# Batch 0 of a clustered-attention and MLP kernel: pieces placed by a table, and another start of head 0

## The chip, the cores and the metric

The kernel runs on one core of one Trainium2 chip. The metric is the device time of one execution in microseconds (us). The profile shows five engines of this core: TensorE (PE in the profile, its weight loads as PEld), VectorE (DVE), ScalarE (ACT), GpSimd (POOL) and SyncE (SP, which issues transfers here). In this kernel TensorE's results stand in PSUM tiles, and VectorE and ScalarE copy them to SBUF.

Kernels are compared only within the same rounds. A ratio is the mean time of one kernel's fast runs over the mean of the other's fast runs of the same rounds, so it is not quite the ratio of the medians that stand beside it.

## The reference

```python
q_n, k_n, c_n = (x / (norm(x) + 1e-6) for x in (q, k, centroids))
q_assign = argmax(einsum('bhsd,hcd->bhsc', q_n, c_n), -1)     # 16 clusters per head
k_assign = argmax(einsum('bhsd,hcd->bhsc', k_n, c_n), -1)
scores = q @ k.T / 8;  scores = where(q_assign == k_assign, scores, -1e9)
x = softmax(scores) @ v                    # 4 batches, 8 heads, 768 tokens, 64 wide
out = gelu_exact(x @ w_in) @ w_out         # 3072 tokens, 512 -> 2048 -> 512
```

There are 32 heads (4 batches of 8). Heads 0 to 9 are prepared with transposes on TensorE; later ones use transfers that transpose.

## The kernel before

Each head goes through these pieces. The names in brackets are those of the table that the change brings in.

- **Split** (GpSimd): q and k become a float16 high part and a float16 residual, side by side in `st`.
- **Transposes** (`trq`, `trk`): six on TensorE for each of q and k into a PSUM buffer, which VectorE copies to `T`.
- **Assignment** (`asq`, `ask`): `T` against the normalised centroids on TensorE.
- **One-hots** (`oneh`): on VectorE a sum of two halves, a maximum and a comparison.
- **One-hot rows** (`onep`): six transposes on TensorE and two VectorE writes into 16 extra rows of `T`, so that the score matmul adds a large value where clusters match.
- **Six key chunks** ("slots" (head, chunk)): two score matmuls, one exp on ScalarE. There are two score buffers in PSUM, so TensorE can be one slot ahead.
- **AV** (`av0` to `av5`): six matmuls each, in the next head's slots. Then **norm** on VectorE, and for each pair of heads **fin** (six transposes, one copy).

```python
def asn(i, which, halves=True):          # asq / ask
    ...
    for j in range(N):
        if halves:                       # both centroid halves side by side: 6 matmuls
            nc.tensor.matmul(a_ps[:, j, which], t[:, js], c_all[:, :, chs], start=True, stop=True)
        else:                            # accumulated: 12 matmuls, but no sum on VectorE
            for e in range(2):
                nc.tensor.matmul(a_ps[:, j, which, 0], t[:, js], c_all[:, e, chs],
                                 start=(e == 0), stop=(e == 1))

def onehot(i, halves=True):              # oneh
    ...
    if halves:
        nc.vector.tensor_reduce(out=asum, in_=..., op=ALU.add)      # the sum
    nc.vector.tensor_reduce(out=amax, in_=asum, op=ALU.max)
    nc.vector.tensor_tensor(oh[...], asum, amax..., op=ALU.is_ge)

def scores(i, c):
    s_ps = ps_sc.tile([128, 2, 512], FP32, tag="sc", name="sc_ps")   # ps_sc: two buffers
    for t in range(2):
        nc.tensor.matmul(s_ps[:, t, 0:QB], Ts[i][0:D + C, 1, ...], Ts[i][0:D + C, 0, ...], ...)
    nc.scalar.activation(ps[i][:, c, :], s_ps[...], ACT_FN.Exp, ...)

# ... the start
nc.gpsimd.tensor_tensor(cent_norm, cent_ssq, half, op=ALU.pow)
nc.vector.tensor_sub(sts[0][:, 1, :, D:2 * D], k_raw, sts[0][:, 1, :, 0:D])   # k residual, head 0
tr_pe(0, 0, copy=nc.scalar.copy, ...)
nc.vector.tensor_scalar_add(cent_norm, cent_norm, 1e-6)
nc.vector.reciprocal(cent_rnorm, cent_norm)
nc.vector.tensor_scalar_mul(cent_hl[:, 0], cent_sb..., cent_rnorm)            # "the multiply"
nc.vector.scalar_tensor_tensor(cent_hl[:, 1, 0, :], cent_sb, cent_rnorm, ...)
# ... placing the pieces, in units of a modelled slot time
AVS0 = {2: (0,), 3: (1, 2), 4: (3,), 5: (4, 5)}      # AV pieces of head i-1 in slot (i, c)
at(g(h - 2, 0), tr_pe, h, 0); at(g(h - 2, 2), tr_pe, h, 1)
at(g(h - 2, 4), prep_asn, h); at(g(h - 1, 1), one_pe, h)
```

The transposes, the one-hot rows and all fins but one share one ring of two PSUM buffers (`ps_o`). Assignment has one buffer and AV has one.

The softmax here doesn't subtract the row's maximum and nothing guards it: scores larger than these inputs give would overflow.

Of the kernel before, what the change touches and what calls it, by code (L numbers as in the profile page):

```python
# [9 lines left out]
FP16 = mybir.dt.float16  # L10
AX = mybir.AxisListType
ALU = mybir.AluOpType
# [8 lines left out]
def kernel(  # L21
# [10 lines left out]
    nc = tc.nc  # L32
# [3 lines left out]
    B, H, S, D = q.shape  # L36
    HC, C, _ = centroids.shape
    DM, DF = moe_w_in.shape
    N = S // 128
    NH = B * H  # L40
    QB = S // 2
# [17 lines left out]
    ps_sc = ctx.enter_context(tc.tile_pool(name="ps_sc", bufs=2, space=PSUM))  # L59
    ps_a = ctx.enter_context(tc.tile_pool(name="ps_a", bufs=1, space=PSUM))  # L60
    ps_x = ctx.enter_context(tc.tile_pool(name="ps_x", bufs=1, space=PSUM))
# [34 lines left out]
    def warm(n, cols=512):  # L96
        for _ in range(n):
            nc.tensor.matmul(w_ps[:, 0:cols], ones[:, 0:128], ones[:, 0:cols],  # L98
                             start=True, stop=True)
# [47 lines left out]
    def tr_pe(i, w, copy=None, pool=None):  # L147
        if i not in Ts:
            Ts[i] = t_pool.tile([128, 2, S], FP16, tag="T", name="T")
        st = sts[i]  # L150
        pl, tag = pool or (ps_o, "op")
        t_ps = pl.tile([128, S], FP16, tag=tag, name="tr_ps")
        for j in range(N):
            nc.tensor.transpose(t_ps[:, j * 128:(j + 1) * 128], st[:, w, j, :], ident)  # L154
        (copy or nc.vector.tensor_copy)(Ts[i][:, w, :], t_ps)  # L155
# [18 lines left out]
    sts[1] = st_pool.tile([128, 2, N, 2 * D], FP16, tag="st", name="st")  # L174
    vraws[1] = v1_raw
    nc.gpsimd.tensor_tensor(cent_norm, cent_ssq, half, op=ALU.pow)
    nc.vector.tensor_sub(sts[0][:, 1, :, D:2 * D], k_raw, sts[0][:, 1, :, 0:D])

    tr_pe(0, 0, copy=nc.scalar.copy, pool=(ps_sc, "sc"))
    warm(1, 256)  # L180
    nc.vector.tensor_scalar_add(cent_norm, cent_norm, 1e-6)
    nc.vector.reciprocal(cent_rnorm, cent_norm)
    nc.vector.tensor_scalar_mul(cent_hl[:, 0],
                                cent_sb.unsqueeze(1).to_broadcast([H * C, 2, D]), cent_rnorm)
    nc.vector.scalar_tensor_tensor(cent_hl[:, 1, 0, :], cent_sb, cent_rnorm,
                                   cent_hl[:, 0, 0, :], ALU.mult, ALU.subtract)
    nc.gpsimd.tensor_copy(half[:, 0:1], cent_hl[:, 1, 0, 0:1])
# [3 lines left out]
    def cent_tr():  # L191
        chl_ps = ps_a.tile([128, 2, 128], FP16, tag="asn", name="chl_ps")
        for w in range(2):
            nc.tensor.transpose(chl_ps[:, w], cent_hl[:, w].rearrange("p a d -> p (a d)"),
                                ident)
        nc.vector.tensor_copy(c_all, chl_ps)

    def tr(i):
        st = sts.pop(i)
# [9 lines left out]
    def asn(i, which, halves=True):  # L209
        h = i % H  # L210
        chs = slice(h * C, (h + 1) * C)
        if which == 0:
            asns[i] = ps_a.tile([128, 512], FP32, tag="asn", name="asn_ps")
        a_ps = asns[i][:, 0:2 * NA].rearrange("p (n w l c) -> p n w l c", n=N, w=2, l=2)
        t = Ts[i][:, which]
        for j in range(N):
            js = slice(j * 128, (j + 1) * 128)
            if halves:
                nc.tensor.matmul(a_ps[:, j, which], t[:, js], c_all[:, :, chs],  # L219
                                 start=True, stop=True)  # L220
            else:
# [4 lines that stand above are left out]
    def onehot(i, halves=True):  # L226
        tile_ps = asns.pop(i)
        a_ps = tile_ps[:, 0:2 * NA].rearrange("p (n w l c) -> p n w l c", n=N, w=2, l=2)
        oh = ohs[(i // 2) % NOH]
        if halves:  # L230
            asum = small.tile([128, N, 2, C], FP32, tag="asum", name="asum")
            nc.vector.tensor_reduce(out=asum, in_=a_ps.rearrange("p n w l c -> p n w c l"),  # L232
                                    axis=AX.X, op=ALU.add)
            amax = tile_ps[:, 2 * NA:2 * NA + 2 * N].rearrange("p (n w o) -> p n w o",
                                                               n=N, w=2)
        else:
            asum = a_ps[:, :, :, 0, :]
            amax = small.tile([128, N, 2, 1], FP32, tag="amax", name="amax")
        nc.vector.tensor_reduce(out=amax, in_=asum, axis=AX.X, op=ALU.max)  # L239
        nc.vector.tensor_tensor(oh[:, :, i % 2, :, 0:C], asum,  # L240
                                amax.to_broadcast([128, N, 2, C]), op=ALU.is_ge)
# [40 lines left out]
    def one_first():  # L282
        half_ps = []
        for e in range(2):
            t_ps = ps_o.tile([128, S], FP16, tag="op", name="oh_ps")
            for j in range(N // 2):
                nc.tensor.transpose(t_ps[:, j * 128:(j + 1) * 128],
                                    ohs[0][:, e * (N // 2) + j].rearrange("p a b c -> p (a b c)"),
                                    ident)
            half_ps.append(t_ps)  # L290
        one_q, one_k = half_ps
        T0 = Ts[0][D:D + C]
        nc.scalar.activation(T0[:, 0, QB:S], one_k[0:C, 0:QB], ACT_FN.Copy, bias=0.0,
                             scale=float(VAL))
        nc.vector.tensor_scalar(T0[:, 0, 0:QB], one_q[0:C, 0:QB],
                                float(VAL), None, op0=ALU.mult)
        for o, z in ((0, 128), (128, QB)):
            nc.vector.tensor_scalar(T0[:, 1, o:z], one_q[32:32 + C, o:z],
                                    -1.0, None, op0=ALU.add)
        tr_pe(1, 1, pool=(ps_x, "x"))  # L300
        nc.vector.tensor_scalar(T0[:, 1, QB:S], one_k[32:32 + C, 0:QB],
                                -1.0, None, op0=ALU.add)

# [118 lines left out]
        nc.gpsimd.dma_start(out=w_chunks[n][0], in_=w_chunks[n][1])  # L422


    tr_pe(0, 1, copy=nc.scalar.copy, pool=(ps_sc, "sc"))
    warm(1)
    nc.scalar.copy(sts[1][:, 1, :, 0:D], k1_raw)
    nc.gpsimd.tensor_sub(sts[1][:, 1, :, D:2 * D], k1_raw, sts[1][:, 1, :, 0:D])
    cent_tr()
    nc.vector.tensor_sub(sts[1][:, 0, :, D:2 * D], q1_raw, sts[1][:, 0, :, 0:D])  # L430
    warm(2)
    asn(0, 0, halves=False)
    asn(0, 1, halves=False)
    onehot(0, halves=False)
    warm(1)
    tr_pe(1, 0, copy=nc.scalar.copy, pool=(ps_sc, "sc"))
    one_first()
    split(2, vnow=False)
    load_w(0)
# [15 lines left out]

    WARM = {}
    AVS = {1: (0,), 2: (1,), 3: (2,), 4: (3,), 5: (4, 5)}
    AVS0 = {2: (0,), 3: (1, 2), 4: (3,), 5: (4, 5)}
    FILL = {}

    def slot(i, c):
        if i < NH:
            scores(i, c)
        if i in WARM:
            warm(WARM[i])
        fill(FILL.get((i, c), 2))
        if i >= 1:
            for j in (AVS0 if i < 10 else AVS).get(c, ()):
                av(i - 1, j)
            if c == 5:  # L470
                norm(i - 1)
# [8 lines left out]
    PT = 10  # L480
    FC1 = {(9, 3): 0, (18, 0): 1, (26, 0): 2}
    events = []

    def at(t, fn, *args, **kw):
        events.append((t, len(events), fn, args, kw))
# [33 lines left out]
    def g(i, c):  # L519
        return TS[i, c] + 0.01  # L520

    def prep_asn(h, halves=True):
        asn(h, 0, halves)
        asn(h, 1, halves)
        onehot(h, halves)

    for n in range(1, 8):
        at(T[n] + 0.5, load_w, n)
    sp_t = -3.7
# [8 lines left out]
            at(max(T[pair] - {10: 25.0, 12: 25.0, 14: 35.0}.get(pair, 29.0) + 2.5 * (h % 2), sp_t + 3.5), tr, h)  # L538
    for h in range(NH - 3, NH):
        at(sp_t + 0.04, vcast, h)  # L540
    for h in range(1, NH):
        pair = h - h % 2
        if h == 1:
            at(g(0, 0), asn, h, 0, False)
            at(g(0, 1), asn, h, 1, False)
            at(g(0, 1), onehot, h, False)
            at(g(0, 3), one_pe, h)
        elif h < PT:
            o = 4 if h == 2 else 0
            at(g(0, 4) if h == 2 else g(h - 2, 0), tr_pe, h, 0)  # L550
            at(g(0, 5) if h == 2 else g(h - 2, 2), tr_pe, h, 1)
            at(g(1, 1) if h == 2 else g(h - 2, 4), prep_asn, h, h > 2)
            at(g(h - 1, 1 + o // 2) if h < 11 else g(10, 4), one_pe, h)
        else:
            if pair < 10:
                at(g(pair - 2, 3) if h % 2 else g(pair - 3, 5), prep_asn, h)
                to, tg = T[pair] - g(pair - 2, 5), T[pair] - g(pair - 1, 2)
            else:
                ta, to, tg = (17.5, 12.0, 5.0) if pair >= 12 else (12.5, 7.0, 3.0)
                t0 = T[pair] - ta + 4.0 * (h % 2)  # L560
                at(t0, asn, h, 0)
                at(t0 + 1.2, asn, h, 1)
                at(t0 + 1.21, onehot, h)
            if h % 2 == 1:
                at(T[pair] - to, ohtr, pair)
                at(T[pair] - tg, aug, pair)
    for h in range(0, NH - 2, 2):
        if h < 8:
            at(g(h + 3, 3) if h < 6 else g(9, 1), fin, h, pe=True)
        else:  # L570
            at(T[h + 3] + 0.1, fin, h)

    for t, _, fn, args, kw in sorted(events, key=lambda e: e[:2]):
# [39 lines left out]
```

## Time and profile before

| | before |
|---|---|
| median of 3 runs, us | 302.93 (302.70 to 303.14) |
| span of the profiled run, us | 300.9 |
| first score matmul, us from the start | 9.39 |
| slots (2,0), (4,0), (6,0) start at | 18.92, 29.01, 38.73 |
| first MLP matmul | 55.52 |

"First MLP matmul" means here the first of the main MLP loop (`hp`, L386 in the kernel before). Eight early MLP matmuls (`hp_early`) are spread ahead of it, the first at 50.92 us.

Busy time of each engine in two stretches of the kernel before (the number in brackets counts instructions):

```profile
core 0: us, PE busy (x) PEld busy (x) DVE busy (x) ACT busy (x) POOL busy (x), PEclk, DMA share, GB/s
...
15.00:45.00 30.00, 29.82 (x512) 23.88 (x511) 26.21 (x59) 27.91 (x38) 28.77 (x45) 1.00 1.15 268
60.00:250.00 190.00, 190.00 (x1973) 117.46 (x1972) 71.98 (x171) 148.49 (x186) 53.80 (x85) 1.00 0.60 131
```

From 60 us on TensorE is busy without a break, so a shift of the first stretch should pass to the end. In batch 0 four engines look nearly full. For TensorE this is misleading. The Trainium skill ("TensorE: Matmul & The Clock Gate", section "Wait — 56ns, not 53.3ns?") gives a start-to-start time of 55.6 ns for warm back-to-back matmuls of 128 columns. The trace agrees: transposes recorded at 219 ns start every 55 ns, so most of the recorded time overlaps. A slot can then be summed by starts: two score matmuls 0.32 us, six AV matmuls 0.18, six transposes 0.34, twelve assignment matmuls 0.30.

This is the timeline of TensorE, then of ScalarE, around slot (5,3) of the kernel before. The columns are the start, the time to the end of the merged row, the engine, line, operation and operands, and in brackets the idle time before it and who ended it:

```profile
36.06 0.49 PE L311 MATMUL sc_ps<-T 80*128 80x384 f16 x2
36.39 0.53 PE L326 MATMUL x_ps<-vaug_149,p_sb 128*128 128x65 f16 x12
36.88 0.51 PE L350 MATMUL fin_ps<-ident,x_tok 128*128 128x128 f16 x6
37.22 0.49 PE L311 MATMUL sc_ps<-T 80*128 80x384 f16 x2
```

```profile
34.26 3.14 ACT L314 ACTIVATE p_sb<-sc_ps 128x768 f16<-128x768 f32 x4
37.75 2.37 ACT L314 ACTIVATE p_sb<-sc_ps 128x768 f16<-128x768 f32 x3 [0.35 <-PE sc_ps L311]
```

The slot holds twelve AV matmuls and six transposes. The next pair of score matmuls therefore starts 1.16 us later (36.06 to 37.22), where ScalarE needs a new one every 0.70 us, and ScalarE idles 0.35 us.

The start, on VectorE, in the kernel before:

```profile
3.73 0.56 DVE L163 TENSOR_TENSOR st<-q_raw,st 128x384 f16<-128x384 f32 x1
4.38 0.56 DVE L177 TENSOR_TENSOR st<-k_raw,st 128x384 f16<-128x384 f32 x1
4.85 0.15 DVE L181 TENSOR_SCALAR cent_norm<-cent_norm 128x1 f32<-128x1 f32 x1
5.04 0.16 DVE L182 RECIPROCAL cent_rnorm<-cent_norm 128x1 f32<-128x1 f32 x1
5.24 0.29 DVE L183 TENSOR_SCALAR cent_hl<-cent_sb,cent_rnorm 128x128 f16<-128x128 f32 x1
```

The k residual of head 0 (L177) stands ahead of the centroid chain; the multiply (L183) takes 0.29 us.

### The profile page before, as it was taken

Reading aid. Unit: us, or ns where it says so; the run is one execution under the profiler, and the core shown is the slowest. Engines: PE = TensorE matmul, PEld = TensorE weight load, DVE = VectorE, ACT = ScalarE, POOL = GpSimd, SP = SyncE. Lnnn points to the kernel's source line nnn. Section 1 sums busy time; section 2 is a strip of 40 time slices with the busy share of each in tenths; the row PEclk is TensorE's granted clock in tenths of the full one; section 3 lists DMA queues with packets and bytes.
Section 4 is the critical chain, followed back from the end, with each engine's and each line's share of the span. In section 5 each row is a group of like instructions: output and inputs, shape, how many; then the busy total and the mean of one; then the engine's idle time right before and its main releaser. Section 6 shows DMA issues by size and latency. Waiting matters only on the chain.

```text
span 300.9 us, 7413 instructions
## 1 busy us (share of the span) xinstructions
PE 295.8 (98%) x3109; PEld 186.8 (62%) x3109; DVE 122.8 (41%) x284; ACT 215.2 (72%) x274; POOL 106.6 (35%) x182
## 2 busy tenths in 40 slices
PE   8899999999999999999999999999999999999996
PEld 4678887666666666666566666666566665565444
DVE  5788987103564732122353842223344413000112
ACT  5899999956888888856788888855788883466000
POOL 3999999998033204663522304600000000000000
PEclk9999999999999999999999999999999999999999
DMA  6999999993378369976579436876032231100122
GB/s 232 361 297 254 259 262 210 237 233 87 60 178 206 91 81 238 232 160 178 113 162 197 118 86 209 165 96 131 2 89 54 70 54 44 38 0 0 44 97 70
DMA packets 74065, 42.85 MB, mean 142 GB/s; under 512 B 54320, under 2 KB 71088, under 8 KB 74032
## 3 DMA queue, kind: packets, MB, share of 16 engines
q1 hardware_dynamic: 69520, 38.09, 52.5%
q0 software_dynamic: 4224, 4.19, 8.4%
q8 instruction: 24, 0.39, 0.6%
q10 hardware_dynamic: 288, 0.10, 0.1%
q14 instruction: 9, 0.07, 0.1%
HBM read 27.30 MB, written 6.29 MB: 112 GB/s over the span
## 4 chain that ended last, share of the span: by engine, by line
PE 94%; POOL 2%; DVE 1%; ACT 1%; issue 0%
PE hp L386 27%; PE op L412 24%; PE sc_ps L311 20%; PE x_ps L326 11%; PE op_alt L412 3%; PE asn_ps L219 3%; PE tr_ps L154 2%; PE w_ps L98 1%; PE oh_ps L265 1%; PE fin_ps L350 1%; POOL st L133 1%; ACT p_sb L314 1%; ACT T L155 1%; PE hp_early L367 0%; POOL st L132 0%; POOL st L135 0%
## 5 line engine op out<-in xcount | busy, mean ns | idle before, releaser
L314 ACT ACTIVATE p_sb<-sc_ps 128x768 f16<-128x768 f32 x192 | 148.9, 810 | 21.8 <-PE sc_ps L311 12.9
L311 PE MATMUL sc_ps<-T 80*128 80x384 f16 x384 | 93.7, 325 | 0.7 <-ACT p_sb L314 0.4
L386 PE MATMUL hp<-xt,w_in_sb 128*128 128x384 f16 x504 | 85.0, 326 | 0.0
L326 PEld LDWEIGHTS <-p_sb 128*128 128x128 f16 x1152 | 54.6, 97 | 30.9 <-DVE x_tok L337 0.2
L386 PEld LDWEIGHTS <-w_in_sb 128*128 128x128 f16 x504 | 47.9, 98 | 30.4
L132 POOL CAST st<-q_raw 128x384 f16<-128x384 f32 x30 | 15.3, 509 | 78.7 <-DMA q_raw<-in_q_dram 56.9
L416 DVE COPY o_sb<-op 128x512 f32<-128x512 f32 (+1 forms) x22 | 14.8, 672 | 54.9 <-PE op L412 54.9
L232 DVE TENSOR_REDUCE asum<-asn_ps 128x192 f32<-128x384 f32 x29 | 16.2, 557 | 51.3 <-PE asn_ps L219 51.2
L311 PEld LDWEIGHTS <-T 80*128 80x128 f16 x384 | 26.8, 97 | 5.5 <-issue 1.1
L135 POOL TENSOR_TENSOR st<-k_raw,st 128x384 f16<-128x384 f32 x30 | 27.4, 913 | 2.4
L133 POOL TENSOR_TENSOR st<-q_raw,st 128x384 f16<-128x384 f32 x30 | 27.3, 911 | 2.5
L336 DVE RECIPROCAL rec<-x_ps 128x6 f32<-128x6 f32 x32 | 6.2, 193 | 42.5 <-PE x_ps L326 42.5
L337 DVE TENSOR_TENSOR x_tok<-x_ps,rec 128x384 f16<-128x384 f32 x32 | 17.8, 558 | 1.1
L219 PEld LDWEIGHTS <-T 128*128 128x128 f16 x348 | 14.7, 96 | 4.4
L219 PE MATMUL asn_ps<-c_all,T 128*128 128x32 f16 x348 | 16.7, 177 | 0.0
L134 POOL CAST st<-k_raw 128x384 f16<-128x384 f32 x30 | 15.2, 505 | 0.0
L275 DVE TENSOR_SCALAR T<-ohT 16x768 f16<-16x768 f16 x22 | 8.2, 371 | 8.2 <-DMA ohT<-oh_166 4.0
L154 PE MATMUL tr_ps<-ident,st 128*128 128x128 f16 x120 | 10.6, 227 | 0.3 <-POOL st L133 0.2
L239 DVE TENSOR_REDUCE asn_ps<-asum 128x12 f32<-128x192 f32 x29 | 10.5, 361 | 1.0
L154 PEld LDWEIGHTS <-st 128*128 128x128 f16 x120 | 8.6, 101 | 3.1 <-DVE st L163 0.9
L155 DVE COPY T<-tr_ps 128x768 f16<-128x768 f16 x17 | 9.4, 554 | 0.6
L278 DVE TENSOR_SCALAR T<-ohT 16x768 f16<-16x768 f16 x22 | 9.0, 410 | 0.3
(308 smaller groups left out, 405.4 us busy)
## 6 DMA issues: line engine op xcount, KB each, us to landing
q_raw<-in_q_dram SPq DMA_DIRECT2D x32, 192.0 KB, 4.2
k_raw<-in_k_dram SPq DMA_DIRECT2D x32, 192.0 KB, 4.1
v_raw<-in_v_dram SPq DMA_DIRECT2D x32, 192.0 KB, 4.0
out_dram<-o_sb SPq DMA_DIRECT2D x23, 256.0 KB, 2.3
w_in_sb<-in_moe_w_in_dram POOLq DMA_DIRECT2D x4, 512.0 KB, 9.5
w_out_sb<-in_moe_w_out_dram POOLq DMA_DIRECT2D x4, 512.0 KB, 9.9
T<-st SPq DMA_TRANSPOSE x22, 4.8
xt<-x_tok SPq DMA_TRANSPOSE x11, 2.9
```

What stands on the lines that cost most here:

```text
L132: nc.gpsimd.tensor_copy(st[:, 0, :, 0:D], q_raw)
L133: nc.gpsimd.tensor_sub(st[:, 0, :, D:2 * D], q_raw, st[:, 0, :, 0:D])
L135: keng.tensor_sub(st[:, 1, :, D:2 * D], k_raw, st[:, 1, :, 0:D])
L154: nc.tensor.transpose(t_ps[:, j * 128:(j + 1) * 128], st[:, w, j, :], ident)
L219: nc.tensor.matmul(a_ps[:, j, which], t[:, js], c_all[:, :, chs], start=True, stop=True)
L232: nc.vector.tensor_reduce(out=asum, in_=a_ps.rearrange("p n w l c -> p n w c l"), axis=AX.X, op=ALU.add)
L311: nc.tensor.matmul(s_ps[:, t, 0:QB], Ts[i][0:D + C, 1, c * 128:(c + 1) * 128], Ts[i][0:D + C, 0, t * QB:(t + 1) * QB], start=True, stop=True)
L314: nc.scalar.activation(ps[i][:, c, :].rearrange("p (t q) -> p t q", t=2), s_ps[:, :, 0:QB], ACT_FN.Exp, bias=0.0, scale=float(scale))
L326: nc.tensor.matmul(x_ps[:, j], ps[i][:, ch, j * 128:(j + 1) * 128], va[:, ch, 0:D + 1], start=(ch == 0), stop=(ch == N - 1))
L337: nc.vector.tensor_tensor(xtoks[i - i % 2][:, :, i % 2, :], x_ps[:, :, 0:D], rec.to_broadcast([128, N, D]), op=ALU.mult)
L386: nc.tensor.matmul(hp[:, t, 0:QB], w_in_sb[:, m, f * 128:(f + 1) * 128], xts[b][:, m, t * QB:(t + 1) * QB], start=(m == 0), stop=(m == NM ...
L412: nc.tensor.matmul(op[:, 0:w], gs[b][f][:, js], w_out_sb[:, f, ms], start=(f == 0), stop=(f == NF - 1))
```

## The change

The intent is to fill the slots of batch 0 more evenly and to reach the first score sooner. The AV, transpose, assignment, one-hot, norm and fin pieces of heads 0 to 9 (AV and norm up to head 8) are listed per slot in a table. Head 0's k residual goes to GpSimd so that the centroids come sooner. Head 0's k transposes are evicted in two halves, one by ScalarE and one by VectorE. Head 1's k transposes move into the first slot. Head 2's assignment uses the form with 12 matmuls and a sum. In the diff, `warm(n)` issues n filler matmuls on TensorE whose results nobody reads; a pair of heads, below, is the time from slot (4,0) to slot (6,0).

```diff
-    nc.vector.tensor_sub(sts[0][:, 1, :, D:2 * D], k_raw, sts[0][:, 1, :, 0:D])
+    nc.gpsimd.tensor_sub(sts[0][:, 1, :, D:2 * D], k_raw, sts[0][:, 1, :, 0:D])
...
-    nc.vector.tensor_scalar_mul(cent_hl[:, 0],
-                                cent_sb.unsqueeze(1).to_broadcast([H * C, 2, D]), cent_rnorm)
+    nc.vector.tensor_tensor(cent_hl[:, 0], cent_sb.unsqueeze(1).to_broadcast([H * C, 2, D]),
+                            cent_rnorm.unsqueeze(2).to_broadcast([H * C, 2, D]), op=ALU.mult)
...
+    def tr_halves(i, w):
+        for e, (pl, tag, copy) in enumerate(((ps_sc, "sc", nc.scalar.copy),
+                                             (ps_o, "op", nc.vector.tensor_copy))):
+            ...   # three transposes and a copy of 384 columns each
...
-        tr_pe(1, 1, pool=(ps_x, "x"))
+        tr_pe(1, 0, pool=(ps_x, "x"))
...
-    tr_pe(0, 1, copy=nc.scalar.copy, pool=(ps_sc, "sc"))
     warm(1)
+    cent_tr()
+    tr_halves(0, 1)
     nc.scalar.copy(sts[1][:, 1, :, 0:D], k1_raw)
     nc.gpsimd.tensor_sub(sts[1][:, 1, :, D:2 * D], k1_raw, sts[1][:, 1, :, 0:D])
-    cent_tr()
-    nc.vector.tensor_sub(sts[1][:, 0, :, D:2 * D], q1_raw, sts[1][:, 0, :, 0:D])
-    warm(2)
+    warm(1)
     asn(0, 0, halves=False)
     asn(0, 1, halves=False)
     onehot(0, halves=False)
-    warm(1)
-    tr_pe(1, 0, copy=nc.scalar.copy, pool=(ps_sc, "sc"))
+    nc.vector.tensor_sub(sts[1][:, 0, :, D:2 * D], q1_raw, sts[1][:, 0, :, 0:D])
+    warm(3)
     one_first()
...
+    PLAN = {
+        (0, 0): ((1, 'trk'),),
+        (0, 1): ((1, 'asq'),),
+        (0, 2): ((1, 'ask'), (1, 'oneh'),),
+        ...
+        (4, 0): ((5, 'oneh'), (2, 'norm'), (6, 'trq'),),
+        (4, 1): ((5, 'onep'),),
+        (4, 2): ((3, 'av0'), (3, 'av1'),),
+        (4, 3): ((6, 'trk'), (6, 'asq'),),
+        (4, 4): ((3, 'av2'), (3, 'av3'), (6, 'ask'),),
+        (4, 5): ((3, 'av4'), (3, 'av5'),),
+        ...   # up to (10, 0)
+    }
```

More of the change, by code (lines that the diff above doesn't have):

```diff
@@ L196, in cent_tr @@
         nc.vector.tensor_copy(c_all, chl_ps)
+    def tr_halves(i, w):
+        for e, (pl, tag, copy) in enumerate(((ps_sc, "sc", nc.scalar.copy),
+                                             (ps_o, "op", nc.vector.tensor_copy))):
+            t_ps = pl.tile([128, S], FP16, tag=tag, name="tr_ps")
+            for j in range(N // 2):
+                nc.tensor.transpose(t_ps[:, j * 128:(j + 1) * 128],
+                                    sts[i][:, w, e * (N // 2) + j, :], ident)
+            copy(Ts[i][:, w, e * QB:(e + 1) * QB], t_ps[:, 0:QB])
     def tr(i):
@@ L457 @@
     AVS = {1: (0,), 2: (1,), 3: (2,), 4: (3,), 5: (4, 5)}
-    AVS0 = {2: (0,), 3: (1, 2), 4: (3,), 5: (4, 5)}
     FILL = {}
@@ L466, in slot @@
         fill(FILL.get((i, c), 2))
-        if i >= 1:
-            for j in (AVS0 if i < 10 else AVS).get(c, ()):
+        if i >= 10:
+            for j in AVS.get(c, ()):
                 av(i - 1, j)
@@ L482 @@
     events = []
+    ONE = {1}
+    PLAN = {
+        (0, 0): ((1, 'trk'),),
+        (0, 1): ((1, 'asq'),),
+        (0, 2): ((1, 'ask'), (1, 'oneh'),),
+        (0, 3): ((2, 'trq'),),
+        (0, 4): ((1, 'onep'),),
+        (0, 5): ((2, 'trk'), (2, 'asq'),),
+        (1, 0): ((3, 'trq'),),
+        (1, 1): ((2, 'ask'), (2, 'oneh'), (3, 'trk'),),
+        (1, 2): ((0, 'av0'), (0, 'av1'),),
+        (1, 3): ((0, 'av2'), (2, 'onep'),),
+        (1, 4): ((3, 'asq'), (3, 'ask'), (0, 'av3'), (3, 'oneh'),),
+        (1, 5): ((0, 'av4'), (0, 'av5'), (0, 'norm'),),
+        (2, 0): ((4, 'trq'),),
+        (2, 1): ((3, 'onep'),),
+        (2, 2): ((1, 'av0'), (1, 'av1'),),
+        (2, 3): ((4, 'trk'), (4, 'asq'),),
+        (2, 4): ((1, 'av2'), (1, 'av3'), (4, 'ask'),),
+        (2, 5): ((1, 'av4'), (1, 'av5'),),
+        (3, 0): ((4, 'oneh'), (1, 'norm'), (5, 'trq'),),
+        (3, 1): ((4, 'onep'),),
+        (3, 2): ((2, 'av0'), (2, 'av1'), (2, 'av2'),),
+        (3, 3): ((5, 'trk'), (5, 'asq'),),
+        (3, 4): ((0, 'fin'), (2, 'av3'), (5, 'ask'),),
+        (3, 5): ((2, 'av4'), (2, 'av5'),),
+        (4, 0): ((5, 'oneh'), (2, 'norm'), (6, 'trq'),),
[4 more added lines that the diff above has]
+        (4, 5): ((3, 'av4'), (3, 'av5'),),
+        (5, 0): ((6, 'oneh'), (3, 'norm'), (7, 'trq'),),
+        (5, 1): ((6, 'onep'),),
+        (5, 2): ((4, 'av0'), (4, 'av1'), (7, 'asq'),),
+        (5, 3): ((7, 'trk'), (4, 'av2'),),
+        (5, 4): ((2, 'fin'), (7, 'ask'),),
+        (5, 5): ((4, 'av3'), (4, 'av4'), (4, 'av5'),),
+        (6, 0): ((7, 'oneh'), (4, 'norm'), (8, 'trq'),),
+        (6, 1): ((7, 'onep'),),
+        (6, 2): ((5, 'av0'), (5, 'av1'),),
+        (6, 3): ((8, 'trk'), (5, 'av2'),),
+        (6, 4): ((5, 'av3'), (8, 'asq'), (8, 'ask'),),
+        (6, 5): ((8, 'oneh'), (5, 'av4'), (5, 'av5'), (5, 'norm'),),
+        (7, 0): ((9, 'trq'),),
+        (7, 1): ((8, 'onep'),),
+        (7, 2): ((6, 'av0'), (6, 'av1'),),
+        (7, 3): ((9, 'trk'), (9, 'asq'),),
+        (7, 4): ((6, 'av2'), (6, 'av3'), (9, 'ask'),),
+        (7, 5): ((6, 'av4'), (9, 'oneh'), (6, 'av5'),),
+        (8, 0): ((6, 'norm'), (4, 'fin'),),
+        (8, 1): ((9, 'onep'),),
+        (8, 2): ((7, 'av0'), (7, 'av1'),),
+        (8, 3): ((7, 'av2'),),
+        (8, 4): ((7, 'av3'), (7, 'av4'),),
+        (8, 5): ((7, 'av5'),),
+        (9, 0): ((7, 'norm'),),
+        (9, 1): ((6, 'fin'),),
+        (9, 2): ((8, 'av0'),),
+        (9, 3): ((8, 'av1'),),
+        (9, 4): ((8, 'av2'), (8, 'av3'),),
+        (9, 5): ((8, 'av4'), (8, 'av5'),),
+        (10, 0): ((8, 'norm'),),
+    }
@@ L520, in g @@
         return TS[i, c] + 0.01
-    def prep_asn(h, halves=True):
-        asn(h, 0, halves)
-        asn(h, 1, halves)
-        onehot(h, halves)
     for n in range(1, 8):
@@ L540 @@
         at(sp_t + 0.04, vcast, h)
-    for h in range(1, NH):
-        pair = h - h % 2
-        if h == 1:
-            at(g(0, 0), asn, h, 0, False)
-            at(g(0, 1), asn, h, 1, False)
-            at(g(0, 1), onehot, h, False)
-            at(g(0, 3), one_pe, h)
-        elif h < PT:
-            o = 4 if h == 2 else 0
-            at(g(0, 4) if h == 2 else g(h - 2, 0), tr_pe, h, 0)
-            at(g(0, 5) if h == 2 else g(h - 2, 2), tr_pe, h, 1)
-            at(g(1, 1) if h == 2 else g(h - 2, 4), prep_asn, h, h > 2)
-            at(g(h - 1, 1 + o // 2) if h < 11 else g(10, 4), one_pe, h)
-        else:
-            if pair < 10:
-                at(g(pair - 2, 3) if h % 2 else g(pair - 3, 5), prep_asn, h)
-                to, tg = T[pair] - g(pair - 2, 5), T[pair] - g(pair - 1, 2)
-            else:
-                ta, to, tg = (17.5, 12.0, 5.0) if pair >= 12 else (12.5, 7.0, 3.0)
-                t0 = T[pair] - ta + 4.0 * (h % 2)
-                at(t0, asn, h, 0)
-                at(t0 + 1.2, asn, h, 1)
-                at(t0 + 1.21, onehot, h)
-            if h % 2 == 1:
-                at(T[pair] - to, ohtr, pair)
-                at(T[pair] - tg, aug, pair)
+    PIECES = {"trq": lambda h: tr_pe(h, 0), "trk": lambda h: tr_pe(h, 1),
+              "asq": lambda h: asn(h, 0, h not in ONE), "ask": lambda h: asn(h, 1, h not in ONE),
+              "oneh": lambda h: onehot(h, h not in ONE), "onep": one_pe,
+              "fin": lambda h: fin(h, pe=True), "norm": norm,
+              **{f"av{j}": (lambda h, j=j: av(h, j)) for j in range(N)}}
+    for (i, c), row in PLAN.items():
+        for n, (h, piece) in enumerate(row):
+            at(TS[i, c] + 0.01 + 0.1 * n, PIECES[piece], h)
+    for h in range(PT, NH):
+        pair = h - h % 2
+        ta, to, tg = (17.5, 12.0, 5.0) if pair >= 12 else (12.5, 7.0, 3.0)
+        t0 = T[pair] - ta + 4.0 * (h % 2)
+        at(t0, asn, h, 0)
+        at(t0 + 1.2, asn, h, 1)
+        at(t0 + 1.21, onehot, h)
+        if h % 2 == 1:
+            at(T[pair] - to, ohtr, pair)
+            at(T[pair] - tg, aug, pair)
     for h in range(0, NH - 2, 2):
-        if h < 8:
-            at(g(h + 3, 3) if h < 6 else g(9, 1), fin, h, pe=True)
-        else:
+        if h >= 8:
             at(T[h + 3] + 0.1, fin, h)
```

## The prediction

> **What bounds the kernel now.** The page's busy line shows TensorE 98%, ScalarE 72%, VectorE 41%, GpSimd 35%. By stage (busy time by stretches) it splits in two. From about 55 us on, TensorE is solid (10.00 of every 10 us, no idle before it): whatever the first 55 us gain should reach the end unchanged. From 9.4 to 55 us (batch 0, heads 0 to 8), VectorE is 90%, ScalarE 94%, GpSimd 96% and TensorE "100%" busy. The last misleads: the Trainium skill ("Trainium Kernel Development and Optimization", Performance Expectations) calls matmul busy time a bad metric because matmuls are pipelined, and here transposes recorded at 219 ns start every 55 ns. By starts, a pair of score matmuls costs TensorE 0.32 us, six AV matmuls 0.18, six transposes 0.34, twelve assignment matmuls 0.30. Added up, the work from the first score (9.39) to the first MLP matmul (55.52) is 41.3 us of 46.1; the exps need 57 x 0.705 = 40.2. So at most about 4 us can be won there.
>
> In steady state a pair of heads takes 9.72 us (29.01 to 38.73). TensorE's own work is 9.0, VectorE's chain (two T copies, two one-hot writes, three assignment steps, two norm steps per head, one xt copy per pair) is 9.07, with 0.41 and 0.24 idle waiting for assignment matmuls. Reordering can take at most 0.65 us per pair.
>
> **What the change does.**
> 1. Start: the k residual of head 0 leaves VectorE (0.56 us) for idle GpSimd (0.91 us as its other residuals there; the skill's "GPSIMD Engine Reference" says roughly 2x slower for two inputs, this trace 1.6x). The centroid chain starts 0.53 us sooner, and the k transposes are evicted in halves by ScalarE and VectorE together. I walk the chain: assignment done 0.5 us sooner, minus about 0.1 for the q1 residual placed before the one-hot writes: first score at 8.95 instead of 9.39.
> 2. Head 1's k transposes move into slot (0,0); head 2's assignment uses 12 matmuls instead of 24 (-0.3 us TensorE) but adds a 0.56 us reduction on VectorE.
> 3. AV, transposes and assignment are spread: no slot holds 12 AV matmuls plus transposes (the 1.16 us slots, ScalarE idle 0.35). But T copies and assignment of one head now come one slot apart, so TensorE will wait about 0.35 us per head for the k copy.
>
> A slot-by-slot sum with these durations gives 55.5 for the kernel before (true: 55.52) and 54.15 after: 0.44 from the start, about 0.5 in heads 0 to 3, about nothing in heads 4 and 5, about 0.4 in heads 6 to 8 where VectorE work ends.
>
> **Prediction: 301.6 us, 300.3 to 302.6 (8 in 10). Faster by over 2%: 0.01; within 2%: 0.98; slower: 0.01.** 2% is 6.1 us, more than the stage has.
>
> **What would show it.** First score about 8.95, first exp 9.5; first MLP matmul about 54.2; end earlier by the same. 1.16 us slots gone, longest near 1.2 in the fourth or fifth slot of a head, with waits on VectorE's T copy. VectorE over 92% busy from 15 to 45 us. A head pair near 9.6 us.
>
> **What would make it wrong.** If the waits on T copies are shorter (VectorE queues better than I sum), up to 2.5 us. If raw loads or GpSimd's splits of heads 2 and 3 hold transposes, or the half evictions don't overlap, the start's gain vanishes. If weights or fin transposes gate the MLP, the gain is given back there.

## The result, and the profile after

| | before | after |
|---|---|---|
| median of 4 runs, us | 303.01 (302.70 to 303.14) | 302.18 (301.94 to 302.27) |
| ratio, 95% interval | | 0.9973, 0.9956 to 0.9990 |
| first score matmul, us | 9.39 | 9.43 |
| slot (4,0) | 29.01 | 28.73 |
| slot (6,0) | 38.73 | 38.37 |
| first MLP matmul | 55.52 | 54.76 |
| end of the profiled span | 300.95 | 300.16 |

The change is 0.83 us faster by the medians, inside the predicted range; 1.3 us was the predicted centre. That is 0.3%: far below the 2%, but the interval leaves 1 out. The shift at the first MLP matmul (0.76 us) reaches the end (0.79 us): nothing was given back later.

The stretches of the changed kernel:

```profile
core 0: us, PE busy (x) PEld busy (x) DVE busy (x) ACT busy (x) POOL busy (x), PEclk, DMA share, GB/s
...
15.00:45.00 30.00, 29.48 (x502) 23.16 (x500) 26.82 (x60) 28.44 (x38) 28.84 (x45) 1.00 1.16 273
60.00:250.00 190.00, 190.00 (x1971) 117.34 (x1970) 73.98 (x172) 148.95 (x185) 54.53 (x85) 1.00 0.59 132
```

The start, on VectorE and on GpSimd, in the changed kernel:

```profile
4.28 0.15 DVE L181 TENSOR_SCALAR cent_norm<-cent_norm 128x1 f32<-128x1 f32 x1
4.47 0.16 DVE L182 RECIPROCAL cent_rnorm<-cent_norm 128x1 f32<-128x1 f32 x1
4.66 0.83 DVE L183 TENSOR_TENSOR cent_hl<-cent_sb,cent_rnorm 128x128 f16<-128x128 f32 x1
5.53 0.28 DVE L185 SCALAR_TENSOR_TENSOR cent_hl<-cent_sb,cent_rnorm,cent_hl 128x64 f16<-128x64 f32 x1
...
8.08 0.67 DVE L443 TENSOR_TENSOR st<-q_raw,st 128x384 f16<-128x384 f32 x1
```

```profile
4.44 0.91 POOL L177 TENSOR_TENSOR st<-k_raw,st 128x384 f16<-128x384 f32 x1 [0.21 <-ACT st L172]
```

The chain does start 0.57 us sooner (4.28 against 4.85). But the multiply that took 0.29 us now takes 0.83, beside the GpSimd subtraction that was moved away from VectorE, and the next op starts at 5.53, against 5.56 before. The gain of 0.57 us shrinks to 0.03.

The steady part, slot (4,4) of the changed kernel, on TensorE, its weight loads, VectorE and ScalarE:

```profile
31.69 0.48 PE L320 MATMUL sc_ps<-T 80*128 80x384 f16 x2
32.01 0.53 PE L335 MATMUL x_ps<-vaug,p_sb 128*128 128x65 f16 x12
32.69 0.32 PE L228 MATMUL asn_ps<-c_all,T 128*128 128x32 f16 x6
32.85 0.48 PE L320 MATMUL sc_ps<-T 80*128 80x384 f16 x2
```

```profile
32.68 0.22 PEld L228 LDWEIGHTS <-T 128*128 128x128 f16 x6 [0.27 <-DVE T L155]
```

```profile
30.91 0.56 DVE L276 TENSOR_SCALAR T<-oh_ps 16x768 f16<-16x768 f16 x1
31.48 0.56 DVE L278 TENSOR_SCALAR T<-oh_ps 16x768 f16<-16x768 f16 x1
32.07 0.56 DVE L155 COPY T<-tr_ps 128x768 f16<-128x768 f16 x1
33.04 0.56 DVE L241 TENSOR_REDUCE asum<-asn_ps 128x192 f32<-128x384 f32 x1 [0.41 <-PE asn_ps L228]
```

```profile
33.37 2.27 ACT L323 ACTIVATE p_sb<-sc_ps 128x768 f16<-128x768 f32 x3 [0.35 <-PE sc_ps L320]
```

The fin transposes have left the slot with twelve AV matmuls, yet the slot again lasts 1.16 us (31.69 to 32.85) and ScalarE again idles 0.35 us. TensorE waits for VectorE's k copy, which stands behind two one-hot writes. VectorE then waits 0.41 us for the assignment of that same k. Seen on each engine these are two waits; they are one hand-over and its answer.

### The profile page after: what moved, and what is told of

It is laid out like the page before. It is cut to its first block, busy times and chain, and to the rows that moved or that the text cites. A ratio compares the mean times of both kernels' runs of the same rounds, so it can differ in the third digit from the quotient of the medians.

```text
span 300.2 us, 7392 instructions
## 1 busy us (share of the span) xinstructions
PE 295.1 (98%) x3098; PEld 185.6 (62%) x3098; DVE 125.2 (42%) x286; ACT 214.0 (71%) x273; POOL 108.1 (36%) x183
## 4 chain that ended last, share of the span: by engine, by line
PE 89%; DVE 6%; ACT 3%; DMA 1%; issue 0%
PE hp L395 27%; PE op L421 25%; PE sc_ps L320 18%; PE x_ps L335 10%; PE op_alt L421 3%; ACT p_sb L323 3%; PE asn_ps L228 3%; PE tr_ps L154 1%; DVE T L155 1%; DMA q_raw<-in_q_dram 1%; DVE T L276 1%; DVE T L278 1%; DVE x_tok L346 1%; PE fin_ps L359 1%; DVE asum L241 1%; DVE oh L249 0%
## 5 line engine op out<-in xcount | busy, mean ns | idle before, releaser
L421 PE MATMUL op<-w_out_sb,g 128*128 128x512 f16 (+1 forms) x352 | 97.1, 371 | 0.0
L400 ACT ACTIVATE g<-hp 128x768 f16<-128x768 f32 x63 | 51.1, 811 | 37.2 <-PE hp L395 37.1
L335 PEld LDWEIGHTS <-p_sb 128*128 128x128 f16 x1152 | 53.7, 97 | 29.8 <-DVE x_tok L346 0.6
L335 PE MATMUL x_ps<-vaug,p_sb 128*128 128x65 f16 x1152 | 58.5, 193 | 0.0
L421 PEld LDWEIGHTS <-g 128*128 128x128 f16 x416 | 38.9, 97 | 30.2
L228 PEld LDWEIGHTS <-T 128*128 128x128 f16 x360 | 15.6, 96 | 5.5 <-DVE T L155 0.8
L228 PE MATMUL asn_ps<-c_all,T 128*128 128x32 f16 x360 | 18.0, 177 | 0.4 <-DVE T L155 0.2
L143 POOL CAST vaug<-v_raw 128x384 f16<-128x384 f32 x32 | 16.1, 508 | 0.0
L284 DVE TENSOR_SCALAR T<-ohT 16x768 f16<-16x768 f16 x22 | 9.4, 428 | 6.9 <-DMA ohT<-oh 6.4
```

Source lines behind the costliest of these rows:

```text
L143: nc.gpsimd.tensor_copy(va[:, :, 0:D], vraws.pop(i))
L335: nc.tensor.matmul(x_ps[:, j], ps[i][:, ch, j * 128:(j + 1) * 128], va[:, ch, 0:D + 1], start=(ch == 0), stop=(ch == N - 1))
L400: nc.scalar.activation(g.rearrange("p (t q) -> p t q", t=2), hp[:, :, 0:QB], ACT_FN.Gelu, bias=0.0, scale=1.0)
L421: nc.tensor.matmul(op[:, 0:w], gs[b][f][:, js], w_out_sb[:, f, ms], start=(f == 0), stop=(f == NF - 1))
```

## The experiments

Each table of this section gives the median in us, its range, and the ratio to the kernel before of the same rounds. Every kernel's output passed the comparison with the reference, also the two that are less exact.

### First round: which part of the start, and is it the table?

**The changed kernel again**, as a yardstick.

> The changed kernel once more, as the yardstick for the three others of this call. Both theories: 0.997 of the kernel before (0.7 to 0.9 us faster), first score at 9.4 us, first MLP matmul at 54.8, and the VectorE multiply that makes the normalised centroids at about 0.83 us.

**The multiply with a pointer scalar**, as before the change:

```diff
-    nc.vector.tensor_tensor(cent_hl[:, 0], cent_sb..., cent_rnorm..., op=ALU.mult)
+    nc.vector.tensor_scalar_mul(cent_hl[:, 0], cent_sb..., cent_rnorm)
```

> The changed kernel with one line put back: the centroid multiply on VectorE takes its scalar by a pointer (one tensor input) as in the kernel before, no longer as two tensor inputs; the GpSimd residual stays. Theory A (the two-input VectorE op waits for the two-input GpSimd op that runs beside it): the multiply takes 0.29 us, not 0.83; cent_hl is ready about 0.5 us sooner, but TensorE's filler matmuls hold the centroid transposes until about 5.7, so the first score comes 0.2 to 0.3 us earlier than in the changed kernel (about 9.15) and the whole about as much. Theory B (the two-tensor form is slow by itself) expects the same here; the run k_vector tells them apart. Theory C (the slow multiply is hidden by TensorE's fillers): first score unchanged at 9.4.

**The k residual back on VectorE**, the two-tensor multiply kept:

```diff
-    nc.gpsimd.tensor_sub(sts[0][:, 1, :, D:2 * D], k_raw, sts[0][:, 1, :, 0:D])
+    nc.vector.tensor_sub(sts[0][:, 1, :, D:2 * D], k_raw, sts[0][:, 1, :, 0:D])
```

> The changed kernel with head 0's k residual back on VectorE, the two-tensor multiply kept. Theory A: with GpSimd idle beside it the multiply takes about 0.29 us. Theory B: it takes 0.83 us here too, and the first score comes at 9.9 or later. Under A the first score is at 9.3 to 9.5, that is the move to GpSimd bought nothing.

**The table alone**: the whole start of the kernel before, with the table less its entry `(0, 0): ((1, 'trk'),)`, which the old start does before the loop.

> The start of the kernel before (its order, evictions, centroid multiply and residual on VectorE, head 1 transposed before the loop) with the new table of pieces. If the table alone carries the gain: as fast as the changed kernel or up to 0.2 us faster, first score at 9.4, second head's wait for its one-hot rows (slot 1,0) shorter than 0.4 us. If the new start were worth the 0.44 us I predicted: 0.4 us slower than the changed kernel.

| run | median (range) | ratio, 95% interval | multiply, us | first score | first MLP matmul |
|---|---|---|---|---|---|
| after_again | 302.08 (301.92 to 302.29) | 0.9969, 0.9956 to 0.9981 | 0.88 | 9.41 | 54.72 |
| ts_mul | 301.99 (301.85 to 302.30) | 0.9969, 0.9955 to 0.9982 | 0.82 | 9.38 | 54.69 |
| k_vector | 302.00 (301.94 to 302.01) | 0.9966, 0.9954 to 0.9979 | 0.29 | 9.44 | 54.76 |
| table_only | 301.89 (301.77 to 302.01) | 0.9963, 0.9950 to 0.9975 | 0.29 | 9.34 | 54.66 |

The multiply in `ts_mul`, with one tensor and a pointer scalar, and the GpSimd op beside it:

```profile
4.66 0.82 DVE L183 TENSOR_SCALAR cent_hl<-cent_sb,cent_rnorm 128x128 f16<-128x128 f32 x1
```

```profile
4.49 0.91 POOL L177 TENSOR_TENSOR st<-k_raw,st 128x384 f16<-128x384 f32 x1 [0.29 <-ACT st L172]
```

The multiply in `k_vector`, the same two-tensor form as in the change, with GpSimd idle:

```profile
5.28 0.29 DVE L183 TENSOR_TENSOR cent_hl<-cent_sb,cent_rnorm 128x128 f16<-128x128 f32 x1
```

So the form of the op is not the cause (theory B falls): the one-tensor form is slow too, and the two-tensor form is fast when GpSimd is idle. Theory A stands, but not in the words in which I had put it ("two-input op"). My expectation for `ts_mul`, that the pointer form would escape the collision, was wrong.

All four have the first score within 0.1 us of each other, and their intervals overlap. The new start contributes nothing that these runs can show, and the table carries the gain. "The table" includes head 2's other assignment form, which all four have; which of its moves earns how much was not tested one by one. Nor was the new start run with the old placing.

### Second round: take the collision away, and lighten VectorE

**No k residual for head 0** (wrong): GpSimd writes zeros at an early, idle time, and nobody subtracts.

```diff
+    nc.gpsimd.memset(sts[0][:, 1, :, D:2 * D], 0.0)
...
-    nc.gpsimd.tensor_sub(sts[0][:, 1, :, D:2 * D], k_raw, sts[0][:, 1, :, 0:D])
```

> Wrong on purpose (head 0's k residual is set to zero early by GpSimd and not computed; only near-ties of one head's cluster choice can change). It takes the residual off VectorE and takes away the GpSimd op beside the centroid multiply. Theory A (what the move off VectorE won was given back by the collision of the GpSimd subtraction with the centroid multiply): multiply 0.29 us instead of 0.83, centroid rows ready at 5.3 instead of 5.8, first score 0.25 to 0.4 us earlier than in the changed kernel (9.0 to 9.2), the whole 0.2 to 0.4 us faster than it (0.996 of the kernel before). Theory C (TensorE's filler matmuls or another wait hold the chain anyway): first score 9.35 or later, no gain.

**The residual on VectorE after the centroid ops**: the subtraction of `k_vector`, placed behind the `scalar_tensor_tensor`.

> Correct. The residual back on VectorE but after the two centroid ops, so nothing collides and the centroid chain is early. Theory A: multiply 0.29 us, k transposes at about 5.9, first score 0.1 to 0.3 us earlier than in the changed kernel. Theory C: first score unchanged at about 9.4.

**And head 1's q residual on GpSimd**: in addition,

```diff
+    nc.gpsimd.tensor_sub(sts[1][:, 0, :, D:2 * D], q1_raw, sts[1][:, 0, :, 0:D])
     nc.scalar.copy(sts[1][:, 1, :, 0:D], k1_raw)
...
-    nc.vector.tensor_sub(sts[1][:, 0, :, D:2 * D], q1_raw, sts[1][:, 0, :, 0:D])
```

> Correct. As k_late, and head 1's q residual goes from VectorE, where it stands just before the one-hot writes (0.6 to 0.67 us, started at 8.1), to GpSimd, which idles about 0.8 us at that time. If that subtraction is what holds the one-hot writes: first score another 0.2 to 0.4 us earlier than k_late (about 8.8), and the whole 0.4 to 0.7 us faster than the changed kernel (0.995 of the kernel before). If GpSimd's stream is what holds head 1 to 3, its 0.1 us of delay shows as longer waits at the second and third head and the gain is smaller.

**No sum on VectorE** in batch 0 (less exact):

```diff
-              "oneh": lambda h: onehot(h, h not in ONE), ...
+              "oneh": lambda h: onehot(h, False), ...
```

> Less exact on purpose: for heads 2 to 9 the cluster is chosen from the high half of the centroids alone, so VectorE skips its 0.56 us sum per head; TensorE does the same matmuls. Theory V (in the steady part of batch 0 VectorE's queue is what the slots wait for, and spreading the pieces could only take what TensorE's and VectorE's sums leave): a pair of heads drops from 9.64 us to 9.0 to 9.2 (TensorE's own sum), so 1.5 to 2 us less in the whole. Theory P (TensorE's own bursts bound the slots): the pair stays at 9.5 or more, and the whole gains under 0.5 us.

| run | median (range) | ratio, 95% interval | multiply, us | first score | (4,0) to (6,0) | first MLP matmul |
|---|---|---|---|---|---|---|
| k_none | 301.91 (301.49 to 302.01) | 0.9963, 0.9949 to 0.9976 | 0.29 | 9.18 | 9.63 | 54.50 |
| k_late | 301.90 (301.68 to 302.20) | 0.9963, 0.9951 to 0.9976 | 0.29 | 9.19 | 9.64 | 54.52 |
| k_late_q1 | 302.26 (301.74 to 302.27) | 0.9972, 0.9960 to 0.9985 | 0.29 | 9.75 | 9.64 | 55.06 |
| no_sum | 300.92 (300.88 to 300.93) | 0.9931, 0.9919 to 0.9944 | 0.61 | 9.78 | 9.32 | 53.74 |

`k_none` shows the collision's price in its profile: multiply 0.29 us, first score 0.25 us earlier than in the changed kernel. `k_none` also spares head 0's k transposes the wait for a residual, which could be a rival reason. `k_late` rules it out: it does compute the residual, and finishes it later than the changed kernel (5.78 us against 5.35), and its first score is as early (9.19). Theory C falls with this. In the times of whole executions the price is not resolved: the intervals of both runs overlap that of `after_again`.

The maximum of head 0 came 0.38 us earlier in `k_none` (7.03 against 7.41), but a second collision took part of it. VectorE and GpSimd in `k_none`:

```profile
4.69 0.29 DVE L183 TENSOR_TENSOR cent_hl<-cent_sb,cent_rnorm 128x128 f16<-128x128 f32 x1
...
7.42 0.36 DVE L249 TENSOR_TENSOR oh<-asn_ps,amax 128x192 f16<-128x192 f32 x1
7.70 0.80 DVE L443 TENSOR_TENSOR st<-q_raw,st 128x384 f16<-128x384 f32 x1
8.53 0.35 DVE L304 TENSOR_SCALAR T<-oh_ps 16x384 f16<-16x384 f16 x1
```

```profile
7.17 0.91 POOL L438 TENSOR_TENSOR st<-k_raw,st 128x384 f16<-128x384 f32 x1 [0.55 <-ACT st L437]
8.12 0.74 POOL L132 CAST st<-q_raw 128x384 f16<-128x384 f32 x1
```

Head 1's q residual (L443), 0.56 us in the kernel before, takes 0.80 beside a GpSimd subtraction, and GpSimd's cast behind it 0.74 where it usually takes 0.51. The ends tell what happens. In all ten profiles in which this residual overlapped a GpSimd subtraction that had started first, the residual ended 0.41 to 0.42 us after the subtraction, whenever it had started; and the GpSimd cast that followed ended 0.36 us after the residual. These ops do not share and run slower: the later one waits for the end of the earlier one.

`k_late_q1` missed: it is no faster, and its first score was at 9.75. Within that run the step from the maximum to the first score was 1.92 us, against 1.95 in `k_late`, so taking the q residual off VectorE was worth 0.03 us there: VectorE then idled 0.51 us before the first one-hot write, for TensorE's transposes. The late start came from ahead of that. ScalarE's square of the centroids began at 3.67 us, not at 3.27 as in `k_late`, because the centroid transfer landed later. Nothing in the edit precedes it.

Over all 14 profiles the square began at 3.08 to 3.27 us in eight and at 3.48 to 3.68 in six. The start of the kernel before did not mind: first score 9.39 (square at 3.08), 9.34 (`table_only`, 3.53), 9.44 (`search_old` below, 3.64), since VectorE does the k residual while it waits. The changed start had its first score at 9.38 to 9.43 in the four profiles where the centroids were early, and at 9.77 and 9.78 in the two where they were late (`k_first` below and `no_sum`). Here is ScalarE in the changed kernel, then in `k_first`:

```profile
3.23 0.26 ACT L170 ACTIVATE cent_sq<-cent_sb 128x64 f32<-128x64 f32 x1 [0.56 <-DMA cent_sb<-in_centroids_dram]
```

```profile
3.67 0.26 ACT L170 ACTIVATE cent_sq<-cent_sb 128x64 f32<-128x64 f32 x1 [0.99 <-DMA cent_sb<-in_centroids_dram]
```

That the landing time is the cause is read off these profiles. No run set it on purpose, and why it has two values stays open. The timed runs of `k_late_q1` (301.74 once, 302.21 to 302.27 four times) have the same gap of about 0.45 us.

`no_sum` gave the largest step of this round, although its profiled run had late centroids. Its slot (4,4), with the same TensorE pieces:

```profile
31.45 0.48 PE L320 MATMUL sc_ps<-T 80*128 80x384 f16 x2
31.78 0.53 PE L335 MATMUL x_ps<-vaug,p_sb 128*128 128x65 f16 x12
32.15 0.30 PE L228 MATMUL asn_ps<-c_all,T 128*128 128x32 f16 x6
32.30 0.48 PE L320 MATMUL sc_ps<-T 80*128 80x384 f16 x2
```

It lasts 0.85 us, not 1.16; the wait for the k copy is gone. The pair takes 9.32 us, not the 9.0 to 9.2 that theory V foretold: with VectorE lightened by 1.1 us a pair, other limits follow at once (slots of about 0.70 us, as fast as the exps go, between others of 0.81 to 0.87 that TensorE's own pieces fill: in that pair its weight loads waited nowhere over 0.1 us). Theory V holds in direction and not in full size.

### Third round: double the suspected cost, and mend the hand-over

**The maximum twice** for heads 2 to 9:

```diff
         nc.vector.tensor_reduce(out=amax, in_=asum, axis=AX.X, op=ALU.max)
+        if 2 <= i < PT:
+            nc.vector.tensor_reduce(out=amax, in_=asum, axis=AX.X, op=ALU.max)
```

> The changed kernel with VectorE's maximum done twice for heads 2 to 9 (0.39 us more of VectorE per head, the same result, nothing else changed). Theory V (VectorE's queue with its two hand-overs to TensorE is the loop that sets the pace): a pair of heads rises from 9.64 to about 10.4 us and the whole by 2 to 3 us, to 304.2 to 305. Theory P (TensorE's bursts): the 0.35 us that VectorE idles per head swallow it, pair under 9.8, the whole up by less than 0.7 us.

**The k copy ahead of the one-hot writes**, from slot (2,1) to (7,5). For head 6 the table becomes

```diff
-        (4, 1): ((5, 'onep'),),
-        (4, 2): ((3, 'av0'), (3, 'av1'),),
-        (4, 3): ((6, 'trk'), (6, 'asq'),),
-        (4, 4): ((3, 'av2'), (3, 'av3'), (6, 'ask'),),
-        (4, 5): ((3, 'av4'), (3, 'av5'),),
+        (4, 1): ((6, 'trk'),),
+        (4, 2): ((3, 'av0'), (5, 'onep'),),
+        (4, 3): ((3, 'av1'), (6, 'asq'), (6, 'ask'), (6, 'oneh'),),
+        (4, 4): ((3, 'av2'), (3, 'av3'),),
+        (4, 5): ((3, 'av4'), (3, 'av5'), (3, 'norm'),),
```

> The changed kernel with another table from slot (2,1) on: a head's k copy goes on VectorE before the one-hot writes of the head ahead of it (its k transposes move two slots forward, the one-hot transposes one slot back), so the one-hot writes (1.16 us) cover the time in which TensorE does the assignment that VectorE waits for. If VectorE's idle and TensorE's wait for the k copy are one and the same exposed hand-over: the wait (0.31 us in the slots (2,4), (4,4), (6,4)) goes, a pair of heads takes 9.2 to 9.3 us, the first MLP matmul comes 0.7 us earlier than in the changed kernel (about 54.0), the whole is at 301.4 (0.9945 of the kernel before). If the pace is set by something else: no more than 0.2 us.

**A table found by trial against the slot sum**, with the start of `k_late`, and then with the start of the kernel before. It keeps the idea of `k_first` (for example `(3, 0)`: head 5's q transposes, `(3, 1)`: its k transposes, `(3, 2)`: head 4's one-hot rows) and also moves heads 2 and 3 earlier: `(0, 1): ((2, 'trq'), (1, 'asq'))`, `(0, 2): ((1, 'ask'), (1, 'oneh'), (2, 'trk'))`, `(0, 5): ((3, 'trq'), (2, 'asq'), (2, 'ask'))`, `(1, 2): ((2, 'onep'),)`.

> The start of k_late and a table found by moving pieces by hand rule and trial against the slot sum (durations from the traces): by the sum the first MLP matmul comes 1.6 us earlier than with the changed kernel's table, and 0.2 us more from the start if the centroids land early. Expected 300.2 to 300.8 (0.992 of the kernel before). If pairs of heads stay above 9.2 us the sum misses something in VectorE's or GpSimd's stream.

> The same table with the start of the kernel before. If the start is worth nothing where the centroids land late (0.4 to 0.5 us later in two of the profiles so far), this is as fast as search_late within 0.2 us and its own times spread less.

| run | median (range) | ratio, 95% interval | first score | (4,0) to (6,0) | first MLP matmul |
|---|---|---|---|---|---|
| two_max | 304.90 (304.67 to 304.97) | 1.0067, 1.0053 to 1.0081 | 9.39 | 10.42 | 57.47 |
| k_first | 301.68 (301.36 to 301.87) | 0.9960, 0.9947 to 0.9972 | 9.77 | 9.30 | 54.55 |
| search_late | 301.45 (301.33 to 301.54) | 0.9954, 0.9941 to 0.9966 | 9.62 | 9.31 | 54.15 |
| search_old | 300.81 (300.58 to 300.85) | 0.9931, 0.9917 to 0.9944 | 9.44 | 9.31 | 53.56 |

`two_max` shows that VectorE's queue is on the path: 0.39 us more of VectorE per head moves a pair from 9.64 to 10.42 us, exactly twice 0.39. None of VectorE's idle time swallowed it (1.02 us in the pair in the changed kernel, 1.03 us here), and TensorE's waits for VectorE's one-hots in that pair grew from 0.2 to 1.1 us. Theory P falls. The doubled op stands between two hand-overs, so the run alone does not tell VectorE's own sum from the loop through TensorE.

`k_first` shows that the idle time and the wait go together, as one hand-over would. (Its table also moves AV, norm and assignment pieces, so it tests the order as a whole.) VectorE in `k_first`, the same part of head 6's preparation as shown above for the changed kernel:

```profile
30.25 1.01 DVE L155 COPY T<-tr_ps 128x768 f16<-128x768 f16 x2
31.49 0.56 DVE L276 TENSOR_SCALAR T<-oh_ps 16x768 f16<-16x768 f16 x1 [0.23 <-PE oh_ps L274]
32.08 0.56 DVE L278 TENSOR_SCALAR T<-oh_ps 16x768 f16<-16x768 f16 x1
32.66 0.56 DVE L241 TENSOR_REDUCE asum<-asn_ps 128x192 f32<-128x384 f32 x1
```

The sum now follows the one-hot writes without idle time, TensorE no longer waits for the k copy, and a pair takes 9.30 us with the same 20 VectorE instructions. In the whole the profile gained 0.2 us rather than 0.7 over the changed kernel at the first MLP matmul, for two reasons. Its centroids were late (first score 0.34 us later). And at the seam of the two tables, slot (2,2) lasted 1.30 us, because TensorE waited there 0.41 us for head 0's norm and then, as I read it, for a transpose buffer to come free. The whole was expected at 301.4 us; the median is 301.68, with two of the five executions at 301.36 and 301.38 and the profiled one, with its late centroids, at 301.75.

`search_old` is the fastest exact kernel. `search_late` has the same table and lost 0.6 us to it before slot (2,0) (19.55 against 18.96): 0.18 at the first score, with late centroids, and the rest within head 0. There the newer start still transposes head 1's k inside the loop, and slots (0,0) and (0,1) together last 1.90 us against 1.40; that this is the reason is my reading. Both expectations missed: `search_late` was to reach 300.2 to 300.8 us, and `search_old` to equal it within 0.2 us and to spread less (it spreads 0.27 us, `search_late` 0.21). The slot sum was too hopeful for this table: it promised 1.6 us less than the changed kernel's table to the first MLP matmul. From first score to first MLP matmul, `search_late` took 0.80 us less than the changed kernel and `search_old` 1.21.

## Why the prediction was right or wrong

**Right in size class, range and carry.** The range held 302.18, and the shift at the first MLP matmul reached the end. The sum for the stage behind the start was nearly right as well: 54.15 was predicted for the first MLP matmul; moved by the 0.48 us by which the first score missed (9.43 in place of 8.95) that is 54.63, and 54.76 was measured. The range held because it was wide: one of the four terms came to nothing and another to two thirds.

**The mis-sized term: the start.** I predicted "first score at 8.95 instead of 9.39", and 9.43 was measured. The term of 0.44 us was -0.04. The step that failed is "The centroid chain starts 0.53 us sooner" being worth its size. The chain did start 0.57 us sooner, but the residual that was moved to "idle GpSimd" ran at the same time as the multiply and stretched it from 0.29 to 0.83 us. Showing this took `ts_mul`, `k_vector` and `k_none` together. The Trainium skill says it plainly: "GPSIMD Engine Reference", section "1. Specifications", has GpSimd's SBUF interfaces shared with VectorE, with contention for VectorE instructions in a 2-port perf mode or with two SBUF inputs. I cited that page for the speed of the subtraction and left this line out. The q1 residual then collided a second time (0.67 us for 0.56). Even without the first collision the first score came only 0.21 us sooner than in the kernel before (`k_none`, 9.18), so my walk of the chain was too hopeful besides. The prediction did say that the start's gain might vanish, but for other reasons (late loads, late splits, half evictions that don't overlap).

**The other terms.** From the first score to slot (4,0): 0.5 predicted, 0.32 measured (19.62 us before, 19.30 after). Heads 4 and 5: "about nothing" predicted, 0.08 measured. From slot (6,0) to the first MLP matmul: 0.4 predicted, 0.40 measured (16.79 and 16.39).

**The waits.** "TensorE will wait about 0.35 us per head for the k copy" was right in three heads: slots (2,4), (4,4) and (6,4) last 1.18, 1.16 and 1.11 us; the same slots in `no_sum` last 0.84, 0.85 and 0.81, so the wait is 0.3 us. In other heads it was smaller. The 1.16 us slots are gone where they were, and slots of the same length came back where I expected the longest. I did not foresee slot (0,5), which lasts 1.36 us (1.06 before): TensorE waits 0.50 us at its end for head 1's one-hot rows. The table is the reason and not the new start: `table_only`, with the old start, has the same 1.36 us and the same wait, against what I expected of it. The table places head 1's assignment and its one-hot rows one slot later than the kernel before did.

**What I said the profile would show and it did not.** VectorE "over 92% busy" from 15 to 45 us: it is 89% (26.82 of 30 us). VectorE is in the limiting loop although, in the pair of heads 4 and 5, it waits 0.41 us for an assignment and 0.25 us for the fin transposes; "busy" cannot show a loop through two engines. `two_max` and `k_first` showed it.

**Open.** Which of the collision's conditions holds for the one-tensor multiply of `ts_mul` is not shown by any run. The landing time of the centroids was seen, not controlled. Whether `table_only` is faster than the changed kernel (301.89 against 302.08) is not resolved: the intervals overlap. Which of the table's moves carries which part of its gain was not tested.

## What to carry to other kernels

Before moving an op to an idle engine, look at what the old engine will do at that very time: a subtraction moved from VectorE to GpSimd cost as much as it saved, because the next VectorE op had to wait for its end. When two engines hand work to each other and back, put independent work of the right length between an op and the op that needs the answer: `k_first` took a third of a microsecond from each pair of heads by order alone. A doubled cost that comes through in full, as in `two_max`, shows that an engine's work is on the path better than its busy share does.

## What the Trainium skill lacked or had wrong

- "GPSIMD Engine Reference" names the contention with VectorE but gives no size. Here a VectorE multiply of 128x128 fp32 elements took 0.82 to 0.89 us instead of 0.29 when it started 0.17 to 0.22 us into a 0.91 us GpSimd subtraction (four profiles, of them `ts_mul` with a pointer scalar), and 0.61 when it started 0.44 us into it (`no_sum`, `k_first`). It ended 0.08 to 0.15 us after the GpSimd op each time; GpSimd's own op was not slower.
- The same page does not say that the later op waits for the end of the earlier one, nor that this goes both ways: a GpSimd cast of 128x384 elements took 0.74 to 0.83 us instead of 0.51 when it came behind VectorE's subtraction. The skill does have this elsewhere: "SBUF — State Buffer", section "SBUF: two separate sides", says that whichever op starts first holds the shared ports for its whole length and the other one blocks. The ends in these profiles agree. Only a pointer to that section is missing.
- The same page calls GpSimd roughly 2x slower than VectorE for two-input ops. At 128x384 fp32 elements it was 1.6x (0.91 against 0.56 us).
- No page that I read has the spread of a small transfer's landing: the 128x64 centroids, issued at 0.73 to 0.74 us in all 14 profiles, were used at 3.08 to 3.27 us in eight and at 3.48 to 3.68 us in six.
